# Relu and router weight in one VectorE operation, weight conversion partly on ScalarE and during attention, and rearranged block passages, in a fused attention, mixture-of-experts and cosine feed-forward kernel

## The chip, the cores and the metric

The kernel runs on one core of a Trainium2 chip (trn2). The metric is the device time of one execution in microseconds (us), lower is better. Three runs of the kernel before took 2129.78 to 2132.88 us, with a median of 2130.75 us. The engines have short names in the profile: PE is TensorE (with PEld for its weight loads), DVE is VectorE, ACT is ScalarE, POOL is GpSimd, and SP issues the DMAs.

## The reference, cut to what matters

```
# q, k, v: 4 batches, 8 heads, 576 positions, 64 columns, float32
scores = scale * q @ k^T + bias, causal, window of 128; attn = softmax(scores)
x = (attn @ v), as 2304 tokens x 512

logits = x @ w_gate; P = exp(logits - max)         # 2304 x 8 experts
8 times: rows of P, then columns of P are normalised
for e in range(8):                                  # w1: 512 x 1024, w2: 1024 x 512
    out += P[:, e:e+1] * (np.maximum(x @ w1[e], 0) @ w2[e])

h = out @ w_in                                      # w_in: 512 x 2048, float64
result = (h * np.cos(h)) @ w_out                    # w_out: 2048 x 512, float64
```

The weights w_in and w_out are drawn as float64, so the kernel gets them as pairs of 32-bit words and has to make float32 out of them.

## The kernel before, in words

The work has three parts. Attention goes through 80 groups (16 head pairs with 5 groups of query tiles each), written as one software pipeline: iteration n issues the scores of group n, the exponentials of group n - 1, the normalisation of n - 2, and so on. Then the 2304 tokens are cut into three blocks of 768. The phases are the expert layer for blocks 0, 1 and 2 and the feed-forward layer for blocks 0, 1 and 2. A unit is 256 hidden columns: 32 units in a block of the expert layer, 8 in one of the feed-forward layer.

All large matrix products are made in two parts, a high one (fp32r, a ScalarE copy) and a low one (the rest, a VectorE or GpSimd subtraction), as three matmuls for one. The first product of a unit is a Strassen scheme: seven products of 128x384 instead of eight, in the order 5, 1, 4 (of the unit before), 2, 3, 6, 7, with the sums of inputs in tiles xt and those of weights in wa. Each product is six matmuls. `combos` makes the seven xt tiles of the next block during the last unit of a block: for each, a ScalarE copy and a VectorE subtraction.

In block 0 the second product is made token tile by token tile (`g2`, lines 1062 to 1064, a batch of six tiles with six matmuls each, one batch a unit, one unit later at the place m == 0). In blocks 1 and 2 it is a second Strassen scheme over pairs of units: `couple` runs after each product, counts up, and from the LEADth couple on calls `s_step`, which makes six matmuls (line 976), evacuates its bank into the block's accumulator (line 988 on VectorE, 986 on ScalarE), makes the low part (line 996, VectorE) and the high part (line 1000, ScalarE) of an operand two or three steps ahead, loads its weights (line 1004, SP), and forms a difference in the activations H (line 1009, GpSimd). H is cX for even and hodd for odd pairs. The activations get there from `product`: ScalarE copies (line 869), VectorE additions (line 872), a ScalarE Relu (`relu`, line 890), and a GpSimd product with the router weight (`weigh`, line 887), where the last two are put off by `defer` for two or three couples. The router weight of one expert for a block's tokens, broadcast over partitions, is loaded by `load_p` (line 785) into a part of hX (`Pb`); the rest of hX holds block 0's activations and later the three operand slots (`op_slot`).

The preparation of weights runs in the gaps as generators that `slot` advances by one step each: two slots after products 5, 1, 4, 2 and 7, one after 3 and 6. `convert_f64` makes float32 out of one chunk of w_in or w_out (128 x 512 numbers): its first seven steps are VectorE operations (lines 258, 262, 264, 266, 270, 274, 278), the eighth loads the next chunk, the tenth stores the result. In the kernel before its 32 chunks run in blocks 1 and 2, one in each of three units of four. `prep_ffn` then splits these weights into high and low parts; `prep_a`, `prep_b` and `prep_sb` do it for the expert weights in block 0. Each engine works through its instructions in the order in which they are issued.

## Time and profile before

| | us |
|---|---|
| median of three runs | 2130.75 |
| the profiled execution | 2135.6 |
| its span | 2133.7 |
| TensorE busy (10960 matmuls) | 2030.0 (95%) |
| VectorE busy | 1563.5 (73%) |
| GpSimd busy | 1233.0 (58%) |
| ScalarE busy | 954.3 (45%) |

The profiled execution is one more than the three timed ones; its time holds some 2 us ahead of and behind the span. Attention lasts until about 200 us, block 0 until about 710, block 1 until about 1235, block 2 until about 1765, the feed-forward layer to the end. Busy shares are means over stages of different kind, and an engine that is not the bottleneck may be idle at no cost.

### The profile page before, as it was taken

The page shows a single profiled execution, that of the slowest core. Times are in us where ns is not written, and L with a number is a line of the kernel's source. Part 1 is how long each engine was busy: PE and PEld are TensorE (multiplying, and loading weights), DVE is VectorE, ACT ScalarE, POOL GpSimd, SP SyncE. Part 2 cuts the span into 40 slices and gives each one's busy share as a digit, 9 for nine tenths or more (in the row PEclk, how much of TensorE's full clock was granted, in tenths as well). Part 3 has the DMA queues.
Part 4 walks back from the last instruction along what each step waited for, and adds up shares of the span by engine and source line. Part 5 has one row for each costly group of instructions (what it writes and reads, how often), then busy time and mean ns, then how long its engine had stood idle before and what let it go on. Part 6 is the DMA issues. An engine that isn't in the chain of part 4 may idle for free.

```text
span 2133.7 us, 30785 instructions
## 1 busy us (share of the span) xinstructions
PE 2030.0 (95%) x10960; PEld 1862.1 (87%) x10960; DVE 1563.5 (73%) x2553; ACT 954.3 (45%) x1799; POOL 1233.0 (58%) x1004
## 2 busy tenths in 40 slices
PE   8989899999999799999999999998999999999998
PEld 6657788999998699898999989898999998889897
DVE  5665767677676588888888778888765686756765
ACT  6775344444434244344343443343343344544543
POOL 4344567776767257676577765776675743223222
PEclk9989999999999899999999999999999999999999
DMA  6533688888887588889888868888887764555543
GB/s 145 145 86 92 233 276 307 310 300 303 308 300 285 183 298 310 310 302 322 292 307 321 311 224 299 303 312 307 295 294 265 266 239 159 190 207 187 223 173 114
DMA packets 236217, 538.97 MB, mean 253 GB/s; under 512 B 71872, under 2 KB 147744, under 8 KB 217632
## 3 DMA queue, kind: packets, MB, share of 16 engines
q1 hardware_dynamic: 236064, 537.00, 72.4%
q8 instruction: 87, 1.43, 0.3%
q14 instruction: 66, 0.54, 0.1%
HBM read 383.27 MB, written 153.67 MB: 252 GB/s over the span
## 4 chain that ended last, share of the span: by engine, by line
PE 81%; DVE 11%; issue 3%; DMA 3%; ACT 2%; POOL 1%; SPq 0%; POOLq 0%; DVEq 0%; ACTq 0%
PE gT L976 19%; PE y_moe L840 16%; PE z_moe L840 8%; PE gT L1064 6%; PE gT L1062 6%; PE gT L1063 6%; PE y_ffn L840 4%; PE x_moe L840 4%; PE s L493 2%; PE z_ffn L840 2%; DMA wa<-wd 2%; PE x L585 2%; DVE hX L996 2%; PE x_ffn L840 1%; DVE acc_moe L988 1%
## 5 line engine op out<-in xcount | busy, mean ns | idle before, releaser
L976 PE MATMUL gT<-hX,wbX 128*128 128x384 f32 x2688 | 553.6, 340 | 47.1 <-issue 29.8
L976 PEld LDWEIGHTS gT<-hX,wbX 128*128 128x128 f32 x2688 | 474.0, 190 | 67.3 <-issue 35.7
L840 PE MATMUL y_moe<-xtT_moe,wa 128*128 128x384 f32 x1728 | 355.4, 341 | 1.2 <-ACT s_moe L869 1.2
L988 DVE TENSOR_TENSOR acc_moe<-gT,acc_moe 128x384 f32<-128x384 f32 x432 | 238.0, 552 | 152.8 <-PE gT L976 151.7
L840 PEld LDWEIGHTS y_moe<-xtT_moe,wa 128*128 128x128 f32 x1728 | 311.1, 192 | 4.3 <-ACT s_moe L869 1.9
L1062 PE MATMUL gT<-wbX,hX 128*128 128x512 f32 x672 | 265.5, 395 | 12.6 <-DVE acc_moe L1053 5.5
L1064 PE MATMUL gT<-wbX,hX 128*128 128x512 f32 x672 | 265.5, 395 | 3.0 <-POOL hX L828 2.9
L1063 PE MATMUL gT<-wbX,hX 128*128 128x512 f32 x672 | 265.0, 394 | 0.0
L828 POOL TENSOR_TENSOR hX<-cX,hX 128x768 fp32r<-128x768 f32 x48 | 93.0, 1953 | 270.9 <-ACT hX L826 245.2
L869 ACT ACTIVATE s_moe<-y_moe 128x384 f32<-128x384 f32 x192 | 93.9, 489 | 318.6 <-PE y_moe L840 317.3
L887 POOL TENSOR_TENSOR cX<-cX,hX 128x384 f32<-128x384 f32 (+1 forms) x96 | 140.0, 1462 | 93.4 <-ACT cX L890 78.1
L1009 POOL TENSOR_TENSOR cX<-cX 128x768 f32<-128x768 f32 x64 | 138.0, 2156 | 79.1 <-DVE hX L996 79.1
L887 POOL TENSOR_TENSOR hodd<-hodd,hX 128x384 f32<-128x384 f32 (+1 forms) x96 | 146.8, 1531 | 63.2 <-ACT hodd L890 63.2
L1009 POOL TENSOR_TENSOR hodd<-hodd 128x768 f32<-128x768 f32 x64 | 140.4, 2194 | 50.9 <-DVE hX L996 50.9
L1062 PEld LDWEIGHTS gT<-wbX,hX 128*128 128x128 f32 x672 | 127.9, 190 | 40.1 <-DVE acc_moe L1053 5.9
L1064 PEld LDWEIGHTS gT<-wbX,hX 128*128 128x128 f32 x672 | 127.6, 190 | 31.3 <-POOL hX L828 3.7
L1063 PEld LDWEIGHTS gT<-wbX,hX 128*128 128x128 f32 x672 | 127.9, 190 | 25.6
L790 ACT ACTIVATE hX<-cX 128x768 fp32r<-128x768 f32 x64 | 44.0, 687 | 237.3 <-DVE cX L872 237.3
L1053 DVE SCALAR_TENSOR_TENSOR acc_moe<-gT,prob,acc_moe 128x512 f32<-128x512 f32 x174 | 127.7, 745 | 24.9 <-PE gT L1064 23.8
L996 DVE TENSOR_TENSOR hX<-hodd,hX 128x768 fp32r<-128x768 f32 x112 | 139.7, 1248 | 0.8 <-ACT hX L1000 0.8
L996 DVE TENSOR_TENSOR hX<-cX,hX 128x768 fp32r<-128x768 f32 x112 | 136.8, 1221 | 2.2 <-ACT hX L1000 2.2
L132 POOL TENSOR_TENSOR s<-ra 128x256 f32<-128x256 f32 x80 | 61.7, 771 | 124.0 <-DVE wa L144 123.2
(183 smaller groups left out, 4132.2 us busy)
## 6 DMA issues: line engine op xcount, KB each, us to landing
wa<-wd SPq DMA_DIRECT2D x88, 1792.0 KB, 7.3
wbX<-wdp SPq DMA_DIRECT2D x224, 512.0 KB, 7.3
wd<-wa SPq DMA_DIRECT2D x32, 1792.0 KB, 6.7
wdp<-sb SPq DMA_DIRECT2D x32, 1024.0 KB, 4.4
wdp<-wbX SPq DMA_DIRECT2D x96, 256.0 KB, 4.0
wbX<-wd SPq DMA_DIRECT2D x24, 1024.0 KB, 4.8
ra<-in_moe_w_dram SPq DMA_DIRECT2D x64, 256.0 KB, 7.3
rb<-in_moe_w_dram SPq DMA_DIRECT2D x64, 256.0 KB, 3.5
```

Source lines behind the costliest of these rows:

```text
L828: nc.gpsimd.tensor_tensor(out=h[:, 1], in0=c, in1=h[:, 0].bitcast(F32), op=ALU.subtract)
L840: nc.tensor.matmul(ps[:, :HB], wa[:, wl, WI[m], kc, :], x[:, xl, kc, :], start=start and kc == 0 and n_ == 0, stop=stop and kc == 1 and n_ ...
L869: nc.scalar.activation(out=t["s", i], in_=ps[:, :HB], func=AF.Copy)
L887: nc.gpsimd.tensor_tensor(out=H[:, q, x], in0=H[:, q, x], in1=pb[:, r], op=ALU.mult)
L976: nc.tensor.matmul(ps[:, :HB], w[:, u, wl, d * P:(d + 1) * P], x[:, xl, u, :], start=m in (1, 5, 2) and n_ == 0, stop=m in (4, 3, 2) and n ...
L988: nc.vector.tensor_tensor(out=a, in0=ps[:, :HB], in1=a, op=ALU.add)
L996: nc.vector.tensor_tensor(out=x[:, 1], in0=H[:, q], in1=x[:, 0].bitcast(F32), op=ALU.subtract)
L1009: nc.gpsimd.tensor_tensor(out=H[:, t[0]], in0=H[:, t[1]], in1=H[:, t[2]], op=ALU.subtract)
L1053: nc.vector.scalar_tensor_tensor(out=a, in0=ps, scalar=pe, in1=a, op0=ALU.mult, op1=ALU.add)
L1062: nc.tensor.matmul(ps, hf[f][:, 0, ts], wb[:, f, 0, :], start=f == 0, stop=False)
L1063: nc.tensor.matmul(ps, hf[f][:, 0, ts], wb[:, f, 1, :], start=False, stop=False)
L1064: nc.tensor.matmul(ps, hf[f][:, 1, ts], wb[:, f, 0, :], start=False, stop=f == 1)
```

## The change

Relu and router weight become one VectorE instruction, max(H, 0) * weight (for the quadrant of product 4 straight out of PSUM). Of the chunk conversion, two VectorE steps become one ScalarE Relu with scale 2^23 and bias -896 * 2^23. One generator of chunk conversions runs during iterations 4 to 45 of attention, which is four chunks, with the first load at iteration 2; the other 28 run in five units of eight of blocks 1 and 2. The low part of sb moves from GpSimd to VectorE. At the block passages, `combos` gives way between its ScalarE and its VectorE half, and its 14 steps are spread by two tables over the last unit of a block (11) and the first of the next (3); the last batch of block 0 is cut in two halves, for units 0 and 1 of block 1; the router weight's place in hX moves to its first quarter, so that load_p(0) is issued at the start of block 1; and LEAD is one couple less.

```diff
-            nc.gpsimd.tensor_tensor(out=hl[:, :, 1], in0=raw, in1=hl[:, :, 0].bitcast(F32), op=ALU.subtract)
+            nc.vector.tensor_tensor(out=hl[:, :, 1], in0=raw, in1=hl[:, :, 0].bitcast(F32), op=ALU.subtract)
...
-            nc.vector.tensor_scalar(out=a, in0=a, scalar1=896.0, scalar2=896.0, op0=ALU.max, op1=ALU.subtract)
-            yield
-            nc.vector.tensor_scalar(out=a, in0=a, scalar1=23, scalar2=None, op0=ALU.logical_shift_left)
+            nc.scalar.activation(out=a, in_=a, func=AF.Relu, scale=2.0 ** 23, bias=ebias)
+            yield
             yield
...
                 nc.scalar.activation(out=hi_, in_=s, func=AF.Copy)
+                yield
                 nc.vector.tensor_tensor(out=lo_, in0=s, in1=hi_.bitcast(F32), op=ALU.subtract)
...
+                load_f64(0)
                 for u_ in range(2):
...
-            if early and next(early[0], StopIteration) is StopIteration:
-                early.pop(0)
+            for _ in range(2 if n >= 54 else 1):
+                if early and next(early[0], StopIteration) is StopIteration:
+                    early.pop(0)
+            if 4 <= n < 46 and (chunk or n < 36):
+                if not chunk:
+                    chunk.append(convert_f64(n_f64[0]))
+                    n_f64[0] += 1
+                if next(chunk[0], StopIteration) is StopIteration:
+                    chunk.pop(0)
...
         def Pb(g):
-            o = 2 * 3 * TB + g % 2 * TB
+            o = g % 2 * TB
...
-                def weigh(q, r):
-                    nc.gpsimd.tensor_tensor(out=H[:, q, x], in0=H[:, q, x], in1=pb[:, r], op=ALU.mult)
-
-                def relu(q, src):
-                    nc.scalar.activation(out=H[:, q, x], in_=src, func=AF.Relu)
+                def weigh(q, r, src=None):
+                    nc.vector.scalar_tensor_tensor(
+                        out=H[:, q, x], in0=H[:, q, x] if src is None else src, scalar=0.0, in1=pb[:, r],
+                        op0=ALU.max, op1=ALU.mult,
+                    )
...
-                    defer(2, lambda: relu(both, H[:, both, x]))
-                    defer(3, lambda: weigh(both, both))
+                    defer(2, lambda: weigh(both, both))
...
-                    defer(2, lambda: relu(3, H[:, 3, x]))
-                    defer(3, lambda: weigh(3, 1))
+                    defer(2, lambda: weigh(3, 1))
...
-                    relu(2, ps[:, :HB])
-                    defer(2, lambda: weigh(2, 0))
+                    weigh(2, 0, ps[:, :HB])
...
-            o = k % 3 * 2 * TB
+            o = (1 + k % 3) * 2 * TB
...
-        LEAD = 14 + 4 - 6
+        LEAD = 14 + 3 - 6
...
+        LAST = {5: 1, 1: 2, 4: 1, 2: 1, 3: 2, 6: 2, 7: 2}
+        NEXT = {5: 1, 4: 1, 2: 1}
...
-                        batch()
-                    if (kind, b, u) == ("moe", 1, 0):
-                        load_p(0)
+                        part = {0: range(GPB), 1: range(GPB, TPB)}[u] if (kind, b) == ("moe", 1) else range(TPB)
+                        batch(tiles=part)
...
-                if nx and m not in (5, 4):
+                for _ in range(pace.get(m, 0)):
                     next(nx, None)
...
-            if chunk < 4 * NU2 and not bg and kind == "moe" and (b == 1 and u < NU1 - 6 or b == 2 and u > 0) and u % 4 != 3:
+            if chunk < 4 * NU2 and not bg and kind == "moe" and (b == 1 and u < NU1 - 6 or b == 2 and 0 < u < NU1 - 8) and u % 8 in (0, 2, 3, 5, 7):
```

Left out of the diff: the memset of ebias, load_p(0) and the choice of the pace ahead of the loop over products, and the conditions that count the prepared feed-forward units.

## Rows read from the trace of the kernel before

**Rows 1.** Busy time by stage: stretch, its length, PE, PEld, DVE, ACT, POOL, clock, DMA.
```profile
300.00:655.00 355.00, 355.00 (x1786) 321.76 (x1785) 247.29 (x343) 155.66 (x253) 265.04 (x230) 1.00 0.88 304
655.00:745.00 90.00, 75.81 (x364) 68.03 (x364) 55.64 (x77) 30.35 (x51) 39.93 (x31) 0.91 0.64 229
745.00:1235.00 490.00, 462.33 (x2567) 449.47 (x2565) 409.58 (x532) 204.61 (x365) 341.79 (x231) 0.98 0.86 306
1235.00:1725.00 490.00, 471.28 (x2652) 463.16 (x2653) 380.73 (x511) 201.35 (x347) 321.75 (x208) 0.99 0.80 285
```

**Rows 2.** The chain that ended last, block 1: start, length, what.
```profile
758.36 1.04 PE gT L976 x6
```

**Rows 3.** Time line of VectorE around one stall: start, length, line, instruction.
```profile
828.19 2.19 DVE L274 SCALAR_TENSOR_TENSOR fb<-f,fb 128x512 f32<-128x512 uint32 x1
...
830.77 0.54 DVE L988 TENSOR_TENSOR acc_moe<-gT,acc_moe 128x384 f32<-128x384 f32 x1
```

**Rows 4.** Time line of TensorE at the same stall; idle time in brackets.
```profile
831.41 2.04 PE L976 MATMUL gT<-hX,wbX 128*128 128x384 f32 x6 [2.58 <-issue]
```

**Rows 5.** Groups of VectorE in 745 to 1235 us: count, busy us, mean ns, idle before.
```profile
L988 DVE TENSOR_TENSOR acc_moe<-gT,acc_moe 128x384 f32<-128x384 f32 x200 | 110.1, 551 | 61.0 <-PE gT L976 60.5
L996 DVE TENSOR_TENSOR hX<-cX,hX 128x768 fp32r<-128x768 f32 x56 | 68.7, 1227 | 2.2 <-ACT hX L1000 2.2
...
L258 DVE TENSOR_SCALAR fa<-f 128x512 int32<-128x512 int32 x18 | 28.7, 1592 | 2.0 <-DMA f<-in_moe_w_out_dram 2.0
L266 DVE SCALAR_TENSOR_TENSOR fa<-f,fa 128x512 int32<-128x512 int32 x19 | 25.3, 1334 | 0.7
L262 DVE TENSOR_SCALAR fa<-fa 128x512 int32<-128x512 int32 x18 | 23.9, 1329 | 0.6
L274 DVE SCALAR_TENSOR_TENSOR fb<-f,fb 128x512 f32<-128x512 uint32 x19 | 20.0, 1054 | 0.6
L270 DVE TENSOR_SCALAR fb<-f 128x512 int32<-128x512 int32 x19 | 16.2, 851 | 0.0
L264 DVE TENSOR_SCALAR fa<-fa 128x512 int32<-128x512 int32 x18 | 15.4, 856 | 0.0
L278 DVE SCALAR_TENSOR_TENSOR fb<-fb,fa 128x512 f32<-128x512 f32 x19 | 12.9, 681 | 0.0
```

**Rows 6.** A group of ScalarE, by shape, whole span.
```profile
L808 ACT ACTIVATE ta<-cX,quarter 128x768 f32<-128x768 f32 x48 | 43.2, 930 | 4.6 <-DVE cX L872 4.5
```

**Rows 7.** Costliest groups of the page: GpSimd on the even pairs' tile.
```profile
L887 POOL TENSOR_TENSOR cX<-cX,hX 128x384 f32<-128x384 f32 (+1 forms) x96 | 140.0, 1462 | 93.4 <-ACT cX L890 78.1
L1009 POOL TENSOR_TENSOR cX<-cX 128x768 f32<-128x768 f32 x64 | 138.0, 2156 | 79.1 <-DVE hX L996 79.1
```

**Rows 8.** A group of VectorE, by shape, whole span.
```profile
L791 DVE SCALAR_TENSOR_TENSOR hX<-cX,hX 128x768 fp32r<-128x768 f32 x32 | 49.4, 1543 | 2.5 <-ACT hX L790 2.5
```

**Rows 9.** Instructions of lines 996 and 258: shortest, median and longest in ns.
```profile
L996 DVE TENSOR_TENSOR hX<-cX,hX x112: 942/951/2566, 747.7 to 1727.9; 128x768 fp32r<-128x768 f32 x112
...
L258 DVE TENSOR_SCALAR fa<-f x32: 416/1602/2075, 727.3 to 1504.5; 128x512 int32<-128x512 int32 x32
```

**Rows 10.** Time line of TensorE at the passage from block 0 to 1.
```profile
703.26 0.80 PE L1062 MATMUL gT<-wbX,hX 128*128 128x512 f32 x1 [5.48 <-DVE acc_moe L1053]
...
742.14 2.26 PE L840 MATMUL z_moe<-xtT_moe,wa 128*128 128x384 f32 x6 [7.15 <-DMA wa<-wd]
```

**Rows 11.** Time line of VectorE at the same passage.
```profile
694.53 4.95 DVE L344 TENSOR_TENSOR xtB_moe<-xr,xtB_moe 128x768 fp32r<-128x768 f32 x2
```

**Rows 12.** Time line of SP, which issues the DMAs, at the same passage.
```profile
725.53 0.95 SPq L785 DMA_DIRECT2D hX<-pT  x2
729.94 0.33 SPq L119 DMA_DIRECT2D wa<-wd  x1
```

**Rows 13.** Busy time in a stretch of attention, columns as in rows 1.
```profile
20.00:120.00 100.00, 96.80 (x689) 67.38 (x687) 62.50 (x317) 74.82 (x255) 45.30 (x98) 1.00 0.53 130
```

**Rows 14.** Loads of line 243 (chunks of w_in).
```profile
DMA to landing us min/median/max: 2.8/3.5/12.4
```

More of the change, by code (lines that the diff above doesn't have):

```diff
@@ L68, in tile_attention_moe_cos_ffn @@
     quarter = const.tile([P, 1], F32, name="quarter")
+    ebias = const.tile([P, 1], F32, name="ebias")
     prob = const.tile([P, NTT, E], F32, name="prob")
@@ L614, in tile_attention_moe_cos_ffn @@
         nc.vector.memset(quarter, 0.25)
+        nc.vector.memset(ebias, -896.0 * 2.0 ** 23)
         table = const.tile([P, 1], F32, name="table")
@@ L659, in tile_attention_moe_cos_ffn @@
         early = []
+        chunk = []
+        n_f64 = [0]
         NGR = len(groups)
@@ L1072, in tile_attention_moe_cos_ffn @@
         pre_next = []
+        nx = None
+        LAST = {5: 1, 1: 2, 4: 1, 2: 1, 3: 2, 6: 2, 7: 2}
+        NEXT = {5: 1, 4: 1, 2: 1}
         def begin(n):
@@ L1103, in tile_attention_moe_cos_ffn, with batch @@
         sbq += [prep_sb(0), prep_sb(1)]
-        load_f64(0)
-        chunk = ready = 0
+        chunk, ready = n_f64[0], 0
         queue = []
-        rest = []
-        def batch(ticks=1):
-            m = queue.pop(0)
-            for tt in range(TPB):
+        def batch(ticks=1, tiles=range(TPB)):
+            m = queue[0]
+            for tt in tiles:
                 g2(steps[m], tt)
                 if tt == TPB - 1:
+                    queue.pop(0)
                     begin_b(m + 2)
@@ L1135, in tile_attention_moe_cos_ffn @@
                     feed.append(stages(nxt, xr[nxt[1]]))
-            nx = None
+            if (kind, b, u) == ("moe", 1, 0):
+                load_p(0)
+            pace = NEXT if nx else {}
             if last and nxt:
@@ L1139, in tile_attention_moe_cos_ffn @@
                     step_all(feed)
+                pace = LAST
                 nx = combos(nxt, xr[nxt[1]] if nxt[0] == "moe" else accs["moe", nxt[1]])
@@ L1156, in tile_attention_moe_cos_ffn @@
                         product(steps[n - 1], 4)
-                    for x in rest:
-                        next(x, None)
-                    rest.clear()
                     begin(n + 1)
@@ L1171, in tile_attention_moe_cos_ffn @@
                     slot()
-                if nx and m not in (5, 4):
+                for _ in range(pace.get(m, 0)):
                     next(nx, None)
-            if nx:
-                next(nx, None)
-                rest.append(nx)
+            if pace is NEXT:
+                nx = None
             if kind == "ffn" or not b:
@@ L1180, in tile_attention_moe_cos_ffn @@
                 load_p((b - 1) * E + u // UPE + 1)
-            if chunk < 4 * NU2 and not bg and kind == "moe" and (b == 1 and u < NU1 - 6 or b == 2 and u > 0) and u % 4 != 3:
+            if chunk < 4 * NU2 and not bg and kind == "moe" and (b == 1 and u < NU1 - 6 or b == 2 and 0 < u < NU1 - 8) and u % 8 in (0, 2, 3, 5, 7):
                 bg.append(convert_f64(chunk))
                 chunk += 1
-            if ready < NU2 and 4 * (ready + 1) <= chunk - 1 + (not bg) and not bg2:
+            if b and ready < NU2 and 4 * (ready + 1) <= chunk - 1 + (not bg) and not bg2:
                 bg2.append(prep_ffn(NU1 + ready))
@@ L1188, in tile_attention_moe_cos_ffn @@
                 step_all(pre)
+            assert (kind, b, u) != ("moe", 2, NU1 - 5) or ready == NU2 and not bg2
         product(steps[-1], 4)
```

## The prediction, made before the changed kernel was seen to run

> **What bounds the kernel now.** I read the page's slices first, to find the stages, then the busy time of each engine by stage, then who TensorE waits for, then the costly VectorE groups and the time line around single stalls. The reader should see in the stages [rows 1] that TensorE is the clock of this kernel: it is busy for all 355.00 us of the middle of block 0, but for 75.81 of 90.00 us at the passage from block 0 to block 1, and for 462.33 and 471.28 of 490.00 us in blocks 1 and 2. So the question is how much of its idle time the change gives back.
>
> A group of six matmuls takes 1.04 us of the chain [rows 2], so one costs 0.1733 us. Block 1's 2,567 matmuls, 24 of them short transposes (some 4 us), should last 2,543 x 0.1733 + 4 = 445 us; 45 us are lost. Block 2's 2,652 should last 460; 30 are lost. Together 75 us.
>
> The stalls come once for each chunk of w_in/w_out that VectorE converts. One of them [rows 3, 4]: a conversion step takes 2.19 us at 828.19, an addition and an evacuation queued behind it end at 831.31, and TensorE, idle for 2.58 us, starts at 831.41. The profile calls that "issue", but the start is that of the free bank. Blocks 1 and 2 convert some 31 chunks: 75 / 31 = 2.4 us a chunk.
>
> Why: convert_f64 gives one step at each slot, and slots come two to a product in the first four products (5, 1, 4, 2), so all seven VectorE steps fall into four couples of 2 x 1.04 = 2.08 us, 8.3 us in all. Their mean prices [rows 5] are 1.59 + 1.33 + 0.86 + 1.33 + 0.85 + 1.05 + 0.68 = 7.7 us. To these come, in each couple, one evacuation (0.55) and half of a low part (1.23 / 2), 4.7 us over four, and one addition priced as an evacuation, 0.55. That is 12.9 us of work in 8.3, a backlog of 4.6. As 2.4 us of it reach TensorE, the banks absorb about 2.2. This small sum is what I use for the change.
>
> **The change, part by part.** *Conversion.* Two of the seven steps (1.33 + 0.86) leave VectorE for one Relu of 128x512 on ScalarE, 0.93 us at most by a 128x768 with a bias [rows 6], on an engine busy for 204.61 of 490 us [rows 1]. ScalarE waits in it for the step before, still in VectorE's queue; behind it stand the high parts, used two couples later, and the copy after product 1, four couples ahead of product 6 that needs it gone. That hides it, and were the cover gone, 28 x 0.93 = 26 us would be the price. VectorE meets the result two slots later. Four chunks move into attention, so 28 instead of 32 are left, in five units of eight instead of three of four.
>
> *Relu and weight.* ScalarE loses three Relus a unit, which nothing waited for, and GpSimd its products, 140.0 us for one of the two H tiles and as much for the other [rows 7], so 140 us a block. VectorE gains three instructions a unit: one of 128x768 and one of 128x384 with both inputs in SBUF, and one of 128x384 that reads PSUM. The nearest row is the same operation at L791, 1.54 us for 128x768 [rows 8]; I take 0.85 for the 384 in SBUF, half of that and a little, and the evacuation's 0.55 from PSUM. Free prices are lower: a 128x768 low part takes 0.94 at its least and 2.57 at its most, a conversion step 0.42 and 2.08 [rows 9]. I put the difference down to GpSimd at work beside them: it is busy 341.79 of 490 us (70%), and without its products 202 (41%).
>
> So the same sum has two ends. At today's prices: 4.7 + 0.55 + five steps of 5.5 + 0.85 + 0.55 = 12.1, a backlog of 3.8, to which product 7's couple adds 0.55 + 1.16 + 1.54 - 2.08 = 1.2; of 5.0, 2.8 reach TensorE, and 28 chunks cost 78 us, no better than 75. At free prices: (0.55 + 0.47) x 4 + 0.55 + 2.9 + 1.1 = 8.6, backlog 0.3, product 7 adds 0.4; 0.7 is absorbed and nothing reaches TensorE. (Its steps are two of 0.42 and three of 0.68, which L278 takes.) Between the ends I go by GpSimd's load, 41 against 70: 0.7 + 0.58 x 4.3 = 3.2, of which 1.0 reaches TensorE. 28 x 1.0 = 28 us in place of 75: **-47 us**, with ends of -75 and +3.
>
> Here a rule speaks against the change. The rows first: the evacuation, with one input in PSUM, keeps its 0.55 us, while the low part with two inputs in SBUF goes from 0.94 to 2.57 [rows 5, 9]. The Trainium skill, "SBUF — State Buffer", section "Who interferes with whom", says that such an instruction contends with a GpSimd instruction that reads SBUF, and that whoever starts second is blocked for all of the other. By it the new instructions put VectorE more often into that queue; by rows alone I let them have the mean excess of GpSimd's lower load. What the full block would cost is the third rival.
>
> *Block passages.* At the passage 0 to 1 TensorE is idle for 90.00 - 75.81 = 14.2 us, and its granted clock is 0.91 [rows 1], so part of it ran at the lower of the two levels, 1.2 GHz: 8 us at most went there. The first of two long gaps [rows 10], 5.48 us, waits for an evacuation behind a pair of VectorE subtractions that took 4.95 us [rows 11]; splitting ScalarE's and VectorE's half of each combination and starting one product earlier takes those waits apart. The second, 7.15 us, waits for wa: its load is issued at 729.94 [rows 12], and its first use is five products (5.2 us) later. Two things change: load_p(0), which held SP until 725.53 because its target was a buffer still in use, gets a free one and is issued first; and half of the last batch, 18 matmuls of 128x512 at 0.1733 x 512 / 384 = 0.23 us, 4.1 us, moves into that unit. The load then has 9.3 us for a landing that took 12.2 here; a rest of 3 us may stay. Of 14.2 idle and some 4 us of slow clock I take 12 back: **-12 us** (ends -18 and -4). The earlier start of the second chain by one couple moves work and removes none: nothing.
>
> *Low part of sb on VectorE.* 32 instructions of 128x1024, 1.3 to 2.1 us each by the 768 rows scaled. VectorE is busy 247.29 of 355 us there and TensorE never waits: nothing. If that cover failed, 32 x 2 us would show. GpSimd's copy of it no longer holds up VectorE.
>
> *Attention.* Four chunks add 4 x (2.9 to 5.5) = 12 to 22 us to VectorE, busy 62.50 of 100 us in this stretch, while TensorE is at 96.80 [rows 13]: most is covered. ScalarE gets four Relus, SP the chunks' loads (five, of 512 KB) and four stores, each behind and ahead of head loads. Behind each first step stand the maxima that release the score banks, and that step waits for a load issued three groups, some 7 us, earlier. Landing took 2.8 to 12.4 us for the loads of w_in [rows 14]. I take **+5 us** (0 to +27).
>
> *Other passages, feed-forward, first units:* the same split of combinations, where waits are short; nothing.
>
> Sum: -47 - 12 + 5 = -54 us. The profiled execution took 2135.6 us, 4.85 above the median of 2130.75, so the sum is 2081.6 against that one and **2077 us** against the median.
>
> **The rivals.** *VectorE stays as late* (0.20): in every chunk unit it still has more than 14.56 us of work, and the stall stays at 2.4 us a chunk. For it: the means above were taken with products in the same places. Against: two steps fewer in the peak. 28 x 2.4 = 67, a gain of 8; with -12 and +5 it gives 2116.
>
> *Attention pays* (0.10): a first step waits for its load, the banks stay full, and TensorE stands as at the passage, 5.48 us idle and an estimated 3.5 lost at the lower clock behind it, for three of the four chunks: 27 instead of 5, which gives 2099. For it: the one load of 12.4 us. Against: the median of 3.5 us.
>
> *GpSimd blocks the new products* (0.06), the case on the other side: the two instructions with both inputs in SBUF start behind GpSimd's subtractions in H, 2.16 us each [rows 7]. At 1.2 us each above the price taken, three quarters of 2.57 - 0.94 [rows 9], a unit has 2.4 us more. A chunk unit then has seven evacuations (3.9), 3.5 low parts (3.9), three additions (1.7), the products (2.6 + 2.4) and five steps (4.4): 18.9 us against 14 x 1.04 = 14.56. The same count before, 17.5 with seven steps, is 2.9 too many and cost 2.4; 4.3 too many cost 3.6, and 28 times that is 101. 101 - 75 - 12 + 5 = +19, so 2150. It decides from about 0.9 us each, a mean of 2.2 us for the 128x768 product, where the sum crosses zero. For it: the most that the low part took. Against: L996, in the same place, keeps a mean of 1.2 us [rows 5].
>
> The forecast has 0.64. Its own range is 2055 to 2100. To hold 8 in 10 the range takes in attention's rival and the late VectorE: 2055 to 2118. About 0.2%, 4 us, is what a measurement of this kernel can tell from no change. Faster: the forecast and the first two rivals but for their worst ends, 0.91; slower: 0.05 of the third; the same, 0.04.
>
> **What would show it.** Right: gaps of TensorE once a chunk at or below 1 us in blocks 1 and 2, with busy time of 475 us or more in a stretch of 490; the 128x768 product near 1.2 us; low part's mean near 1.1; no DMA wait over 3 us at the passage; attention's end within 5 us of now. Wrong: the "issue" gaps stay at 2 us, the product's mean is above 2.2 us, or TensorE shows waits for the score maxima with a lower clock before 110 us.

## The result and the profile after

The changed kernel takes 2080.3 us (median of four runs, 2079.26 to 2082.25), beside 2130.27 us (2127.67 to 2132.88) for the kernel before, measured with it: a ratio of 0.9766, with a 95% interval of 0.975 to 0.9783. The profiled execution has a span of 2077.5 us, 56.2 less than the 2133.7 of before.

Busy time by stage, columns and order as in [rows 1], with the stretches moved to where the stages now lie; the last line answers to [rows 13]. Line numbers differ from kernel to kernel; the tile names tell which instruction is meant.

```profile
650.00:735.00 85.00, 82.51 (x415) 75.17 (x415) 66.30 (x90) 32.48 (x57) 42.08 (x35) 0.98 0.78 278
735.00:1225.00 490.00, 475.92 (x2700) 470.76 (x2699) 417.75 (x601) 169.14 (x294) 200.90 (x135) 0.99 0.83 308
1225.00:1715.00 490.00, 477.29 (x2709) 471.50 (x2708) 406.57 (x592) 166.72 (x279) 176.24 (x114) 0.99 0.80 292
20.00:120.00 100.00, 95.63 (x671) 67.00 (x669) 70.65 (x329) 75.53 (x251) 46.04 (x94) 1.00 0.60 161
```

TensorE has lost 2.5 us instead of 14.2 at the passage and 14.1 and 12.7 us instead of 27.7 and 18.7 in the two stretches of blocks 1 and 2. GpSimd is down to 41% there, VectorE up a little. The groups of VectorE in block 1 answer to [rows 5] (line 997 is 988 of before, 1005 is 996, 259 is 258; 899 is the new product):

```profile
L1005 DVE TENSOR_TENSOR hX<-cX,hX 128x768 fp32r<-128x768 f32 x55 | 74.1, 1348 | 0.0
L1005 DVE TENSOR_TENSOR hX<-hodd,hX 128x768 fp32r<-128x768 f32 x56 | 71.7, 1280 | 0.0
L899 DVE SCALAR_TENSOR_TENSOR cX<-cX,hX 128x768 f32<-128x768 f32 x16 | 19.0, 1188 | 0.0
L899 DVE SCALAR_TENSOR_TENSOR hodd<-hodd,hX 128x768 f32<-128x768 f32 x16 | 16.5, 1030 | 0.0
L266 DVE SCALAR_TENSOR_TENSOR fa<-f,fa 128x512 int32<-128x512 int32 x15 | 16.1, 1075 | 1.8 <-ACT fa L263 1.8
...
L274 DVE SCALAR_TENSOR_TENSOR fb<-f,fb 128x512 f32<-128x512 uint32 x15 | 11.9, 794 | 0.5
L278 DVE SCALAR_TENSOR_TENSOR fb<-fb,fa 128x512 f32<-128x512 f32 x15 | 10.2, 683 | 0.0
...
L270 DVE TENSOR_SCALAR fb<-f 128x512 int32<-128x512 int32 x15 | 7.7, 513 | 0.0
L259 DVE TENSOR_SCALAR fa<-f 128x512 int32<-128x512 int32 x15 | 6.2, 414 | 0.0
```

The product costs 1.19 and 1.03 us for 128x768. The conversion steps are cheaper, the first by far: 0.41 us in place of 1.59. The low parts are not: 1.35 and 1.28, where 1.23 stood. What TensorE waited for in blocks 1 and 2 (us, times, longest), in the changed kernel and then in the one before:

```profile
PE z_moe L852 <- DMA wa<-wd: 16.5, 10, 2.9
PE gT L985 <- DVE acc_moe L997: 3.1, 5, 1.0
PE gT L985 <- DVE hX L1005: 1.3, 2, 1.0
```

```profile
PE gT L976 <- issue: 29.8, 20, 2.6
PE gT L976 <- DVE acc_moe L988: 5.4, 10, 0.9
```

The 20 stalls called "issue", those of [rows 4], are gone but for one of 0.4 us. A wait that hardly existed (1.6 us in three) has come: ten times TensorE stands for wa, the weights of the next unit. One of them on TensorE's time line, and the granted clock (third column from the right) of the stretch behind it:

```profile
849.97 2.26 PE L852 MATMUL z_moe<-xtT_moe,wa 128*128 128x384 f32 x6 [2.90 <-DMA wa<-wd]
```

```profile
850.00:855.00 5.00, 5.00 (x16) 5.00 (x17) 1.51 (x3) 1.53 (x3) 0.73 (x1) 0.50 0.94 363
```

TensorE is idle for 2.90 us, and for the next 5 us it has the lower of its two levels: 16 matmuls where 5 / 0.1733 = 29 fit. That happens behind four of the ten waits. In the 10 us from 849, 914, 1337 and 1402 us the granted clock averages 0.66, 0.66, 0.83 and 0.83, so it costs another 10 us beside the waits.

To see where the time went, I cut the span at SP's issues of wa's load: the first (in the last unit of block 0), the fifth (in block 1's fourth unit) and the 65th (in block 2's last unit). The middle piece holds 60 units; at 14 groups of 1.04 us each [rows 2] and 4 us of transposes they would last 878 us.

```
us                          to 1st   1st-5th   5th-65th   to the end   span
before                       690.6     69.9      952.3       420.9    2133.7
changed                      689.8     57.4      914.4       416.0    2077.5
predicted change              +5       -12       -47           0
measured change               -0.8     -12.5     -37.9        -4.9     -56.2
```

The runs below have the same table. Its first column scatters: 689.7 to 696.1 us in eight profiles with the same attention (one of them with a small difference in block 0), so a few us there tell nothing.

### The profile page after: what moved, and what is told of

It is laid out like the page before. It is cut to its first block, busy times and chain, and to the rows that moved or that the text cites. A ratio compares the mean times of both kernels' runs of the same rounds, so it can differ in the third digit from the quotient of the medians.

```text
span 2077.5 us, 30570 instructions
## 1 busy us (share of the span) xinstructions
PE 2008.0 (97%) x10960; PEld 1853.6 (89%) x10960; DVE 1608.7 (77%) x2714; ACT 869.5 (42%) x1639; POOL 888.4 (43%) x780
## 4 chain that ended last, share of the span: by engine, by line
PE 81%; DVE 7%; DMA 7%; issue 2%; ACT 1%; POOL 1%; SPq 0%; POOLq 0%; ACTq 0%; DVEq 0%
PE gT L985 19%; PE y_moe L852 17%; PE z_moe L852 9%; PE gT L1073 6%; PE gT L1071 6%; PE gT L1072 6%; DMA wa<-wd 6%; PE y_ffn L852 4%; PE x_moe L852 4%; PE s L494 2%; PE z_ffn L852 2%; PE x L586 2%; PE x_ffn L852 1%; DVE hX L1005 1%; PE T L458 1%
## 5 line engine op out<-in xcount | busy, mean ns | idle before, releaser
L985 PE MATMUL gT<-hX,wbX 128*128 128x384 f32 x2688 | 543.0, 336 | 5.6 <-DVE acc_moe L997 3.1
L852 PE MATMUL y_moe<-xtT_moe,wa 128*128 128x384 f32 x1728 | 347.0, 335 | 0.6 <-ACT s_moe L881 0.6
L852 PEld LDWEIGHTS y_moe<-xtT_moe,wa 128*128 128x128 f32 x1728 | 304.4, 188 | 3.3 <-ACT s_moe L881 0.9
L1018 POOL TENSOR_TENSOR cX<-cX 128x768 f32<-128x768 f32 x64 | 123.3, 1927 | 214.3 <-DVE hX L1005 125.6
L1018 POOL TENSOR_TENSOR hodd<-hodd 128x768 f32<-128x768 f32 x64 | 131.2, 2049 | 195.6 <-DVE hX L1005 109.7
L1005 DVE TENSOR_TENSOR hX<-cX,hX 128x768 fp32r<-128x768 f32 x112 | 148.2, 1323 | 0.9 <-ACT hX L1009 0.9
L852 PE MATMUL z_moe<-xtT_moe,wa 128*128 128x384 f32 x576 | 120.4, 343 | 21.8 <-DMA wa<-wd 16.5
L852 PEld LDWEIGHTS z_moe<-xtT_moe,wa 128*128 128x128 f32 x576 | 102.7, 192 | 27.1 <-issue 7.3
```

Source lines behind the costliest of these rows:

```text
L852: nc.tensor.matmul(ps[:, :HB], wa[:, wl, WI[m], kc, :], x[:, xl, kc, :], start=start and kc == 0 and n_ == 0, stop=stop and kc == 1 and n_ ...
L985: nc.tensor.matmul(ps[:, :HB], w[:, u, wl, d * P:(d + 1) * P], x[:, xl, u, :], start=m in (1, 5, 2) and n_ == 0, stop=m in (4, 3, 2) and n ...
L1005: nc.vector.tensor_tensor(out=x[:, 1], in0=H[:, q], in1=x[:, 0].bitcast(F32), op=ALU.subtract)
L1018: nc.gpsimd.tensor_tensor(out=H[:, t[0]], in0=H[:, t[1]], in1=H[:, t[2]], op=ALU.subtract)
```

## The experiments

### One part of the change taken back

**Relu and weight back on ScalarE and GpSimd** (the deferral of 3 and LEAD with them):

```diff
-                    nc.vector.scalar_tensor_tensor(out=H[:, q, x], in0=..., scalar=0.0, in1=pb[:, r], op0=ALU.max, op1=ALU.mult)
+                    nc.scalar.activation(out=H[:, q, x], in_=src, func=AF.Relu)
+                    nc.gpsimd.tensor_tensor(out=H[:, q, x], in0=H[:, q, x], in1=pb[:, r], op=ALU.mult)
```

> The changed kernel, 2080.3 us, with Relu back on ScalarE, the product with the weight back on GpSimd, and LEAD one couple later. Theory A (GpSimd's operations beside VectorE are what made the conversion steps dear): the first conversion step, 0.42 us in the changed kernel, goes back over 1 us, the step at L278 and the low parts stay or rise, and the time rises by 15 to 40 us, to 2095 to 2120, although VectorE has three instructions a unit fewer. Theory B (only the number of VectorE steps in the four couples counts): the steps keep their prices, VectorE has 2 us a unit less to do, and the time stays within 4 us of 2080 or falls.

Measured: 2077.82 us (ratio to before 0.9765, 0.9736 to 0.9794), no slower than with the part. On the prices theory A was right. VectorE's groups in block 1 with this part back:

```profile
L259 DVE TENSOR_SCALAR fa<-f 128x512 int32<-128x512 int32 x15 | 24.1, 1604 | 0.0
L274 DVE SCALAR_TENSOR_TENSOR fb<-f,fb 128x512 f32<-128x512 uint32 x15 | 17.4, 1162 | 0.5
...
L270 DVE TENSOR_SCALAR fb<-f 128x512 int32<-128x512 int32 x15 | 15.9, 1062 | 0.0
```

The first step is at 1.60 us again, the others at 1.16 and 1.06 against 0.79 and 0.51. On the time it was wrong, and the waits say why:

```profile
PE gT L988 <- DVE acc_moe L1000: 7.4, 12, 1.3
PE z_moe L852 <- DMA wa<-wd: 6.6, 9, 1.9
PE gT L988 <- DVE hX L1008: 6.2, 6, 1.5
```

VectorE's stalls rose from 4.4 to 13.6 us, and those for wa fell from 16.5 to 6.6. The granted clock stays at 1.00 in blocks 1 and 2, too. TensorE arrives later, so the loads have more time: there are two limits side by side, and what one loses the other gives back.

**The exponent's two steps back on VectorE**:

```diff
-            nc.scalar.activation(out=a, in_=a, func=AF.Relu, scale=2.0 ** 23, bias=ebias)
-            yield
+            nc.vector.tensor_scalar(out=a, in0=a, scalar1=896.0, scalar2=896.0, op0=ALU.max, op1=ALU.subtract)
+            yield
+            nc.vector.tensor_scalar(out=a, in0=a, scalar1=23, scalar2=None, op0=ALU.logical_shift_left)
```

> The changed kernel with the exponent's two VectorE steps (maximum and shift) in place of ScalarE's one. Theory B (number of steps): the backlog of a chunk grows by 1.0 to 1.6 us, 27 chunks, so 2107 to 2123. Theory A (GpSimd's load): VectorE has room once the steps are cheap; each of the two costs about 0.5 us, most of which the banks absorb, so under 10 us more, 2080 to 2090.

Measured: 2080.61 us, ratio 0.9787 (0.9753 to 0.9821): nothing, as theory A had it. The waits for wa are 12.7 us here.

**GpSimd kept busy with work that nobody needs**:

```diff
+                def busy():
+                    for _ in range(2):
+                        nc.gpsimd.tensor_tensor(out=wgf, in0=wgf, in1=wgf, op=ALU.mult)
...
+                    defer(3, busy)
+                    defer(3, busy)
```

and one more behind each of the other two products.

> The changed kernel with eight GpSimd products of 128x128 added to each unit of blocks 1 and 2, in place on a constant that nothing reads any more: about as much GpSimd time as the products that the change took away (4.3 us a unit), and nothing waits for it but GpSimd's own queue. Theory A (GpSimd's operations slow those of VectorE that read SBUF alone): the 128x768 product and the conversion steps get longer by 0.2 us or more each, and the time rises by 10 to 30 us. Theory B (their number only): the prices stay within 0.1 us and the time within 4 us of 2080; what it would rise then comes from GpSimd's later subtractions in H.

Measured: 2081.93 us, ratio 0.9782 (0.9747 to 0.9817). Again the prices moved and the time did not. Line 259 from shortest to longest, in the changed kernel, with the idle work beside it, and with the products back on GpSimd:

```profile
L259 DVE TENSOR_SCALAR fa<-f x32: 408/414/438, 20.6 to 1498.0; 128x512 int32<-128x512 int32 x32
```
```profile
L259 DVE TENSOR_SCALAR fa<-f x32: 410/623/1951, 20.0 to 1497.9; 128x512 int32<-128x512 int32 x32
```
```profile
L259 DVE TENSOR_SCALAR fa<-f x32: 416/1594/2070, 19.2 to 1497.4; 128x512 int32<-128x512 int32 x32
```

In the changed kernel each of the 32 steps takes the same 0.41 us, although GpSimd is busy for 41% of the time in block 1. By the time lines it is not this share that decides, but whether a GpSimd instruction is under way when the step starts: that holds for none of the 32 in the changed kernel, for 25 with the idle work, for 28 with the products back and for 30 in the kernel before. One such step of the kernel before, and then a low part of the changed kernel, each with GpSimd's instruction beside it:

```profile
757.33 1.85 POOL L1009 TENSOR_TENSOR cX<-cX 128x768 f32<-128x768 f32 x1
757.64 1.83 DVE L258 TENSOR_SCALAR fa<-f 128x512 int32<-128x512 int32 x1 [1.97 <-DMA f<-in_moe_w_out_dram]
```
```profile
786.66 1.84 POOL L1018 TENSOR_TENSOR cX<-cX 128x768 f32<-128x768 f32 x1 [9.18 <-DVE cX L899]
786.97 2.35 DVE L1005 TENSOR_TENSOR hX<-hodd,hX 128x768 fp32r<-128x768 f32 x1
```

The step ends 0.28 us behind GpSimd's instruction, the low part 0.82 us, and these are the medians of all that start so, too. The Trainium skill, "SBUF — State Buffer", section "Who interferes with whom", says that a tensor_scalar with one source in SBUF may take a mode that uses the port pair shared with GpSimd, and that the one that starts second waits for all of the other. These rows agree. By the same section the low parts, with two inputs in SBUF, are held up as well; with GpSimd's load down from 70 to 41% their mean did not fall. The time lines say why: of the 224 low parts 121 started beside a GpSimd instruction before and took 1.48 us on average; now 88 do, but these take 1.84, for GpSimd's long subtraction (line 1018) has often started just ahead of them. The others take 0.95 us in both kernels.

**Both taken back at once**, the two edits above together:

> The changed kernel with both taken back at once: Relu on ScalarE and product on GpSimd, and the two VectorE steps of the exponent. Either of them alone left the time where it was. Theory E (each is enough by itself: with one back VectorE's couples still fit, with both back the old stall of 2.4 us a chunk returns): 27 chunks of 1 to 2.4 us, some of which the loads' waits give back, so 2100 to 2130. Theory F (neither is the cause of the 38 us won in blocks 1 and 2; the order of the steps, the later LEAD or the passage is): 2080 within 5 us.

Measured: 2089.6 us, ratio 0.9818 (0.9803 to 0.9833): 9 us more than the changed kernel, between the two theories. Eight stalls called "issue" are back, 8.0 us of them. So the two VectorE parts, for which the prediction booked 47 us, are worth 9 in this kernel. Blocks 1 and 2 are still 26 us shorter than before (926.0 against 952.3), and most of that comes from something that the prediction gave no price beyond four chunks fewer, as the next runs show.

### The rate, and the chunks in attention

**No chunks in attention, and three units of four**, as before, with all the rest of the change:

```diff
-            if 4 <= n < 46 and (chunk or n < 36):
...
-                load_f64(0)
...
-            if chunk < 4 * NU2 and ... and (b == 1 and u < NU1 - 6 or b == 2 and 0 < u < NU1 - 8) and u % 8 in (0, 2, 3, 5, 7):
+            if chunk < 4 * NU2 and ... and (b == 1 and u < NU1 - 6 or b == 2 and u > 0) and u % 4 != 3:
```

> The changed kernel without the four chunks converted in attention: all 32 in blocks 1 and 2, three units of four. If a chunk costs what is left of the chunk stalls, 0.3 to 1.0 us, and attention paid nothing for its four, the time is 1 to 4 us longer, 2081 to 2084. If attention paid the 5 us of the prediction, it is 1 to 4 us shorter. If a denser row of chunks brings more of the waits for wa, over 5 us longer.

Measured: 2058.43 us (2055.66 to 2060.31), ratio 0.9672 (0.9644 to 0.97): 22 us faster than the changed kernel, which none of the three expected. Of the 19.7 us between the two profiles 18.3 are in blocks 1 and 2 (896.1 against 914.4 us); attention gives 0.2. In these blocks TensorE waits for wa for 2.1 us in place of 16.5, and the granted clock is 1.00 throughout, so the 10 us of slower clock are gone as well; the waits for VectorE rise by some 3 us.

**Both parts taken back and the old rate**, all three edits above together: what is left of the change is the passages and the low part of sb.

> Both parts taken back and also the chunks in attention and the rate of five units in eight: what is left of the change is the passages and the low part of sb. Theory E (the two parts make the gain, either being enough while the conversions are spread): the blocks go back to the pace of the kernel before, 952 us from block 1's second unit to block 2's end against 914 in the changed kernel, and 2110 to 2120 in all. Theory G (with both back, what the rate does is small, as in the comparison of both-back with the changed kernel): 2085 to 2095.

Measured: 2106.39 us, ratio 0.9907 (0.9874 to 0.994). Blocks 1 and 2 are back at 948.1 us. What TensorE waits for there, with both parts taken back, at the new rate and then at the old one:

```profile
PE gT L989 <- issue: 8.0, 8, 2.6
PE gT L989 <- DVE acc_moe L1001: 7.9, 14, 2.6
```

```profile
PE gT L982 <- issue: 26.8, 18, 2.6
```

With these four kernels the change falls into two pieces that do not add up, the two VectorE parts on one side, the new rate with the early chunks on the other:

```
us, median (5th to 65th load)   parts in          parts taken back    the parts give
new rate, four chunks early     2080.3 (914.4)    2089.6 (926.0)      9
old rate, none early            2058.4 (896.1)    2106.4 (948.1)      48
the new rate gives              -22             17
```

Either takes most of the stalls called "issue" away: of 26.8 us 8.0 are left with the rate alone, 0.3 with the parts alone. Once the two parts have done so, the rate has little left to cure and costs 22 us. Where it helps, it is worth 22.1 us of the middle piece (948.1 - 926.0); four chunks fewer, at (948.1 - 878) / 31 = 2.3 us each, are 9 of these. That the rest lies in how the chunks are spread is likely, but only argued.

### Where the waits for wa come from

Each of the ten waits stands 18 to 21 us behind a load of the weight row (hX<-pT: 384 KB in 768 pieces, each fourth unit), and wa's load, issued 9.1 to 10.6 us ahead of its use, lands after 9.8 to 13.4 us in those units of block 1 and after 6.9 to 9.3 in the others. SP's time line ahead of one such load of wa, in the changed kernel and then at the old rate:

```profile
827.86 0.33 SPq L286 DMA_DIRECT2D w<-fb  x1
828.28 0.52 SPq L216 DMA_DIRECT2D wd<-hla  x1
829.05 0.40 SPq L1013 DMA_DIRECT2D wbX<-wdp  x1
830.48 0.37 SPq L797 DMA_DIRECT2D hX<-pT  x1
831.19 0.54 SPq L216 DMA_DIRECT2D wd<-hlb  x1
831.99 0.53 SPq L1013 DMA_DIRECT2D wbX<-wdp  x1
834.19 0.53 SPq L216 DMA_DIRECT2D wd<-hla  x1
836.47 0.32 SPq L120 DMA_DIRECT2D wa<-wd  x1
```

```profile
825.44 0.44 SPq L790 DMA_DIRECT2D hX<-pT  x1
827.03 0.74 SPq L216 DMA_DIRECT2D wd<-hlb  x1
829.19 0.33 SPq L1006 DMA_DIRECT2D wbX<-wdp  x1
830.27 0.36 SPq L216 DMA_DIRECT2D wd<-hla  x1
834.39 0.33 SPq L120 DMA_DIRECT2D wa<-wd  x1
```

The old rate leaves the unit ahead of the row without a conversion (u % 4 == 3 starts none). The new set holds 3 and 7, so a conversion ends just there, and its store (w<-fb), further stores, or the loads of ra and rb that its end sets off join the row: 2,432 KB in the 9 us ahead of wa here, 1,408 in the other kernel. That load took 13.4 us to land, the one of the other kernel 10.4. Over the 13 loads of wa in blocks 1 and 2 that have a row in the 9 us ahead of them, 1,841 KB are issued in these 9 us and the landing takes 10.7 us on average, at the old rate 1,132 KB and 9.1 us; the loads without a row there land after 7.5 and 7.6 us.

**The row's load behind wa's**, one unit later:

```diff
                     begin(n + 1)
+                    if kind == "moe" and b and u % UPE == 1:
+                        load_p((b - 1) * E + u // UPE + 1)
...
-            elif u % UPE == 0:
-                load_p((b - 1) * E + u // UPE + 1)
```

> The changed kernel with the load of the next weight row (384 KB in 768 pieces, every fourth unit) issued behind the load of wa in the next unit instead of ahead of it. Nine waits of TensorE for wa, 0.6 to 2.9 us each and 16.5 us in all, come about 19 us behind such a load, every 63 us. Theory C (that load holds up wa): the waits fall under 4 us in all, and with the lower clock behind three or four of them (about 3 us each) the time falls by 10 to 20 us, to 2060 to 2070. Rival D (the conversion's and the feed-forward weights' loads and stores fill the DMA engines, and any load waits): the waits stay over 10 us and the time within 4 us of 2080.

Measured: 2070.14 us (2067.76 to 2072.66), ratio 0.9723 (0.9697 to 0.9748): theory C, with no wait for wa left in blocks 1 and 2. A part came back elsewhere:

```profile
PE gT L985 <- DMA wbX<-wdp: 9.7, 9, 3.7
```

Now the pair loads behind the row are late, 9.7 us in nine waits. Even so the 60 units of the middle piece take 899.1 us, 15.3 less than in the changed kernel and 3.0 more than at the old rate, with the new rate and the early chunks still in. So most of what the rate costs there is this meeting of loads, and not the rate as such. Of the 9.9 us by which this profile is longer than the one at the old rate 4.2 are at the passage, where the first late pair load takes 3.7.

**The old rate, and the row behind wa in the unit without a conversion** (the same edit with u % UPE == 0, on the kernel of 2058 us):

> The changed kernel without the chunks in attention (2058 us by itself) and with the load of the weight row behind wa's, in the unit that has no conversion. If the waits for wa that are left there (2.1 us), and the small stalls beside them, come from that load, the time falls by another 2 to 6 us, to 2052 to 2056, with each load of wa landing within 9.2 us; if the row's load only moves the wait to the pair loads behind it, as it did for 7 us in block 1 when it stood behind wa in the next unit, 2057 to 2062.

Measured: 2109.16 us, ratio 0.991 (0.988 to 0.994), a miss by 50 us. SP's waits in blocks 1 and 2, and then TensorE's:

```profile
SPq L790 <- DVE hodd L892: 15.3, 14, 4.4
```

```profile
PE gT L978 <- DMA wbX<-wdp: 39.1, 14, 3.4
```

At that place VectorE has not yet made the product that still reads the row's buffer, and SP stands 14 times, for 1.1 us on average. What is queued behind it is a pair load that is due soon: 39.1 us of waits, and a lower clock behind some of them. One of them on SP's time line, and the start of TensorE that it holds up:

```profile
1267.46 0.37 SPq L790 DMA_DIRECT2D hX<-pT  x1
1267.88 1.11 SPq L1006 DMA_DIRECT2D wbX<-wdp  x2
```
```profile
1280.59 2.26 PE L978 MATMUL gT<-hX,wbX 128*128 128x384 f32 x6 [3.35 <-DMA wbX<-wdp]
```

SP's wait is the smaller part of it: here SP had stood for 0.3 us at most, and TensorE's wait is the longest of all. In the kernel of 2058 us the first pair load behind wa's in these 14 units is issued 0.4 us behind it and takes 8.1 us to land (medians; 7.8 to 10.3). Here the row stands between the two: the pair load is issued 1.7 us behind wa's and takes 11.4 us to land (9.9 to 12.6). So it is late by 1.3 us of issue and 3.3 us of landing, the second behind the row's 768 pieces.

**The same, behind product 3**:

```diff
+                if kind == "moe" and b and m == 3 and u % UPE == 0:
+                    load_p((b - 1) * E + u // UPE + 1)
```

> Without the chunks in attention, and with the load of the weight row two products later than in the try that cost 51 us: behind product 3 of the unit without a conversion, when VectorE's product that it must wait for should be done, so that SP does not stand in it. If SP's wait was what made the pair loads late there, those waits (44.5 us in 15) fall under 8 us, and wa keeps landing within 9.2 us: 2050 to 2060. If the row's own traffic made them late, they stay over 20 us and the time over 2075.

Measured: 2058.28 us, ratio 0.9677 (0.9646 to 0.9709), and 4.2 us of waits for pair loads. The waits went as SP's wait went (one of 4.0 us is left), but the time lines do not put them down to it: the pair load issued 0.5 to 0.7 us behind the row still takes 9.9 to 13.7 us to land. What is new is that another one, issued ahead of the row, lands after 7.9 to 9.7 us, and the one behind the row has more time until its use. There is no gain over the kernel with the old rate alone: with 2.1 us of waits for wa left in it there was nothing to win.

### The passage and the low part of sb

**The old pace of the combinations** (with it the doubled step from group 54 on is taken out):

```diff
                 nc.scalar.activation(out=hi_, in_=s, func=AF.Copy)
-                yield
                 nc.vector.tensor_tensor(out=lo_, in0=s, in1=hi_.bitcast(F32), op=ALU.subtract)
...
-                for _ in range(pace.get(m, 0)):
+                if nx and m not in (5, 4):
                     next(nx, None)
```

> The changed kernel with the combinations of a new block paced as before: both halves of one in one step, starting one product later, one per product. The gap of 5.48 us before the first product of block 1 comes back: 4 to 8 us more with the lower clock behind it at the passage 0 to 1, and under 2 us each at the other four passages: 2084 to 2092 in all. Rival: the wait for wa at the same place hides behind it, and the passage costs no more than 2 us.

Measured: 2086.26 us, but 2075.56 to 2091.81, ratio 0.9792 (0.9754 to 0.983). By the table, 3.5 us are at the passage (60.9 against 57.4), where the gap behind the subtractions grows from 2.5 to 5.1 us; 6.0 more lie ahead of it, inside that column's scatter. Inconclusive by the time, in line by the gap.

**load_p(0) late and the last batch whole**:

```diff
-                        part = {0: range(GPB), 1: range(GPB, TPB)}[u] if (kind, b) == ("moe", 1) else range(TPB)
-                        batch(tiles=part)
+                        batch()
+                    if (kind, b, u) == ("moe", 1, 0):
+                        load_p(0)
```

and the row's buffer back at the end of hX.

> The changed kernel with load_p(0) back in the last batch of block 0, into the buffer that is still in use, and with that batch whole in the first unit of block 1. The wait for wa at the second unit's first product, 7.15 us before and none now, comes back at 3 to 7 us: 2083 to 2089. Rival: with the combinations' gaps gone, SP issues wa's load earlier anyway, and the wait stays under 1 us: 2080.

Measured: 2092.66 us, ratio 0.9832 (0.9801 to 0.9863), 12 us more. Its profile is the fastest of the four runs; there the passage takes 11.1 us more (68.5), with these waits between 690 and 760 us:

```profile
PE y_moe L852 <- ACT s_moe L881: 4.3, 2, 3.6
PE z_moe L852 <- DMA wa<-wd: 3.0, 1, 3.0
```

The granted clock is lower, too: 0.50, 0.50 and 0.66 in the three stretches of 5 us from 730, where the changed kernel has 1.00, which costs some 6.7 us. So 11 of the 12.5 us of the passage are this half, of which wa's wait is only 3.0; with the 3.5 us of the combinations that is more than the whole, so the two overlap.

**The low part of sb back on GpSimd**:

```diff
-            nc.vector.tensor_tensor(out=hl[:, :, 1], in0=raw, in1=hl[:, :, 0].bitcast(F32), op=ALU.subtract)
+            nc.gpsimd.tensor_tensor(out=hl[:, :, 1], in0=raw, in1=hl[:, :, 0].bitcast(F32), op=ALU.subtract)
```

> The changed kernel with the low part of sb back on GpSimd. The prediction costs this at nothing: 2080 within 4 us, with TensorE busy for 348 us or more of the stretch from 300 to 650 us. Rival: GpSimd's 2.4 us instructions hold up VectorE's additions in block 0, and the time rises by over 4 us.

Measured: 2081.98 us, ratio 0.9785 (0.9753 to 0.9818), and TensorE is busy for all 350.00 us from 300 to 650. Nothing, as expected.

### All profiles in one table

```
us                              to 1st   1st-5th   5th-65th   to the end    median
Relu and weight back             696.1     55.8      909.1       418.5    2077.82
two steps back                   693.4     54.9      912.4       417.0    2080.61
GpSimd kept busy                 691.6     57.5      915.1       416.2    2081.93
both back                        692.4     54.9      926.0       417.4    2089.60
old rate, none early             689.6     56.3      896.1       415.8    2058.43
both back, old rate              689.5     56.0      948.1       415.8    2106.39
row behind wa                    690.8     60.5      899.1       417.3    2070.14
old rate, row behind wa          686.2     56.5      948.2       415.7    2109.16
old rate, row behind product 3   690.3     56.3      897.4       417.3    2058.28
old pace of combinations         695.8     60.9      916.0       417.3    2086.26
whole batch, late row            689.8     68.5      911.3       415.6    2092.66
sb's low part on GpSimd          689.7     58.0      914.3       415.5    2081.98
```

## Why the prediction was right, and where it was not

**The total**, 2077 us against 2080.3, holds because its errors cancel in part: the passage is right, the term of the chunks is 9 us too large, and two small terms, +5 and nothing, measured -0.8 and -4.9. As far as that goes it was luck.

*Block passage*, -12: measured -12.5, and the step against the longer gap (load_p(0) ahead, half a batch in the unit) carries 11 of it. The single waits were put down less well: with that half taken back, wa's wait is 3.0 us instead of 7.15, 4.3 us stand for ScalarE's copy after a product, and some 6.7 are lost to the lower clock.

*Conversion, Relu and weight*, -47: measured -37.9. The sum left 28 us of stalls to VectorE; 914.4 - 878 = 36 us are lost now, and most of it not to VectorE: the waits for its evacuations and low parts, which take the place of the stall in [rows 3, 4], are 4.4 us, those for wa 16.5, and the lower clock behind four of these takes 10. (Some 14 of the 75 us before were the lower clock as well: it averages 0.986 over the 952 us of the same piece, and [rows 1] has 0.98 and 0.99. The sum has no term for it and spreads it over the chunks.) The step that failed is the one that cost the rate at nothing but its count ("28 instead of 32 are left, in five units of eight instead of three of four"). The new set of units puts a conversion, and with it its stores and the next loads, into the one unit in four that had none, right ahead of the weight row's load. With VectorE's stall gone TensorE arrives earlier at wa, and the loads are what ends last. The prediction asked what is late next at the passage and did not ask it for the units. With the row's load moved and the rate kept, 15.3 of these 36 us come back. Without the rate these 60 units take 952.3 - 896.1 = 56 us less than before, 52 of them from the two parts (948.1 - 896.1), which leaves 18 us lost where the sum left 28.

*The prices.* The 128x768 product was expected near 1.2 us and took 1.19 and 1.03; TensorE's 475 us of a stretch of 490 are 475.9 and 477.3. That GpSimd's instructions made the conversion steps dear was right: with its products back they cost 1.60, 1.16 and 1.06 us again. The interpolation by GpSimd's load was not: the five steps come to 3.5 us a chunk where it had 4.4 and the free prices 2.9, and the low parts, near 1.1 expected, took 1.28 to 1.35. What counts is which GpSimd instruction is under way at the start, and the share of busy time does not tell that; the mean of the products came out right by luck.

*The rivals.* "VectorE stays as late" is out: one stall called "issue" is left, of 0.4 us. "GpSimd blocks the new products" is out: it needed a mean of 2.2 us. Its mechanism is there, though: 16 of the 64 products of 128x768 start beside a GpSimd instruction and take 1.54 us on average, the other 48 take 0.95. "Attention pays" is out, too: TensorE is busy for 95.6 of 100 us there, 1.2 less than in [rows 13]. The +5 us of the forecast's own term were too many, if anything: five profiles without the four chunks reach the first load of wa at 686.2 to 690.6 us (689.2 on average), eight with them and the new pace of the combinations at 689.7 to 696.1 (691.7), a difference of 2.5 us, within the scatter.

*Feed-forward and other passages*, nothing: measured -4.9 us. It stays with every part taken back (415.5 to 418.5 us in all runs). Two pieces of it can be read from the traces: the waits for VectorE's acc_ffn in this stretch are 2.4 us before, 0.8 in the changed kernel and 2.3 with the old pace of the combinations; and in the kernel before the granted clock is 0.83 in the 10 us from 1768, 1.7 us. The rest stays open.

**Which version.** The change without its new rate and its chunks in attention, 2058.4 us, beats both kernels: a ratio of 0.9672 to the kernel before, where the change as it is has 0.9766. A rate of five units in eight that leaves the unit ahead of the row's load free, with the four early chunks kept, was not tried.

## What to carry to other kernels

Two edits that cure the same stall are not worth the sum of what each cures: take one back at a time, then both, before either is kept, for the one that is no longer needed may cost. When an engine's stall goes, list the loads that were given time by it, with their slack and their landing, and see what else is queued in the same few microseconds. A load that is moved on SP's queue is moved past other loads; look first which load will stand right behind it and how much time that one has, and whether the instruction that frees the moved load's target has run by then. And before an engine's prices are taken to follow another engine's load, look in the time line at what is under way when the dear ones start.

## What was not expected of the hardware

A step of VectorE with a single input in SBUF (line 259, 128x512) took 0.41 us in all 32 cases of the changed kernel, none of which started beside a GpSimd instruction, and 1.60 us on average in block 1 with GpSimd's products back, a factor of four; it then ends 0.28 us behind the GpSimd instruction that was under way at its start. The kernel's time did not change by it (2077.82 against 2080.3 us). And behind a wait of 2.90 us for one load TensorE's granted clock was 0.50 for 5 us, in which it made 16 matmuls instead of 29: 13 x 0.1733 = 2.3 us lost on top of the wait.
